# Three attention units of one batch tied behind products of the second expert, in a two-expert kernel

## The chip, the cores and the metric

The kernel runs on one core of one Trainium2 chip. The metric is the time of one execution on the device, in microseconds (us). A core has five engines with a queue each that is worked in order: TensorE (PE in the profile, its weight loads PEld), VectorE (DVE), ScalarE (ACT), GpSimd (POOL) and SyncE (SP), which here issues nearly all DMAs. TensorE's granted clock has two levels, 1.2 and 2.4 GHz; the profile gives it as a share of the higher one.

## What is computed

Attention with a threshold on four batches of 576 tokens, and then two experts, one after the other, on all 2304 tokens:

```python
scores = scale * np.matmul(q, k.transpose(0, 1, 3, 2))        # 4 batches, 8 heads, 576 x 576
thresh = np.max(scores, axis=-1, keepdims=True) - tau
scores = np.where(scores >= thresh, scores, -1000000000.0)
attn = np.exp(scores - max) / (sum + 1e-09)                    # by row
x = np.matmul(attn, v)                                         # 2304 x 512 in all
# first expert, w_in 512 x 2048, w_out 2048 x 512
h = x @ w_in
P = a[0] + a[1] * h + a[2] * h2 + a[3] * h3
Q = 1.0 + np.abs(b[0]) * np.abs(h) + np.abs(b[1]) * h2
x = (P / (Q + 1e-06)) @ w_out
# second expert
h = x @ w_in
g = np.where(h >= 1, h, np.where(h <= -1, 0.0, (h + 1) ** 2 / 4))
out = g @ w_out
```

## The kernel before

Every operand of a product is split into a high and a low half in float16, and a product is made of three: high by high, high by low, low by high.

**The steps.** After the first batch's attention (a form of its own, some 180 us at the start) the experts run as a list of 192 steps. A step is (expert m, batch b, third j of the batch's 576 tokens, chunk i of 256 columns of the 2048): 24 steps are one expert on one batch, and the list alternates, first expert on batch 1, second expert on batch 1, first expert on batch 2, and so on. In this text steps are numbered 0 to 191 and batches 1 to 4 (the code's b is 0 to 3, its m is 0 or 1). So steps 0 to 23 are the first batch's first expert, 24 to 47 its second expert, 48 to 71 the second batch's first expert.

A step has a first product (`first_product`, L889: 24 matmuls of 192 columns into a bank `ph`, of which there are two), elementwise work on its result, and a second product (`second_product`, L905: 24 matmuls into `acc`), which is made LAG = 3 steps later. The elementwise work of the first expert is `rational`: about four ACT operations and five on DVE (L748 to L761; for the first batch one of them goes to ACT, L757, and one to POOL, L758). That of the second expert is `quadratic`: one on ACT (L812), two on DVE (L813, L814). Both end with `split`: a cast on ACT (L210) and a subtraction on POOL (L214).

**Attention of batches 2 to 4.** `attention(b)` is a generator of 17 units: three that prepare (loads, splitting and transposing of q, k and v), then for each of four pairs of heads three units of three rows (`att_rows`), with one more preparation after the second unit of the first two pairs. So a batch has 36 rows of 128 queries. A row goes through all engines in turn: scores on PE (L397 and L398: 4 matmuls, 8 for the last row of a pair) into one PSUM tile `s` of which there is one buffer; scaled and reduced out of it on DVE (L445), bias on ACT (L446), exponential on ACT (L404), threshold on DVE (L405), cast on ACT (L413), low half on POOL (L414, and L416 twice), a transposing DMA on SP (L418: `eT` from `hl`, three buffers each), and the weighted sum on PE (L431: 14 matmuls of 65 columns and less into `pv`). Two rows end in one `normalize` (L466 to L480, with a PE transpose at L471).

**What sets the order.** The code is traced under priorities (`at(t)`: the work of step t), and a list scheduler then fixes each engine's order, priorities and readiness by its own model deciding: work whose operands are ready may be put far ahead of its step where the model sees an engine free. `ATTENTION` (L39) gives for each batch the steps at which the three preparing units begin, at which its rows begin, and at which they end; `spread` puts the units at even distances between. For batch 2 that was 18, 23.65 and 50. A unit traced for step t gets the priority of t - 1.5 (L975 to L977).

**The weights.** The 8 chunks of an expert's weights stay in SBUF (`wc`, 1 MB each, 8 buffers). When the last third of a batch is through with chunk i of one expert, `load_chunk` (L279) loads chunk i of the other one into its place.

## Time and profile before

| | |
|---|---|
| three runs | 1229.77, 1233.0, 1233.4 us (median 1233.0) |
| profiled execution | 1231.83 us, span from first to last instruction 1230.0 us |
| busy share of the span | PE 89%, PEld 80%, DVE 79%, ACT 68%, POOL 45% |
| granted clock, mean | 0.965 |

The rows used are quoted in a section below. They read like this. A row of the windows view gives, for a stretch of the span in us, the busy time of each engine with the number of its instructions, the granted clock and the DMA engines' share. A row of the groups view gives line, engine, operation, tiles written and read, shape, count, then busy us and mean ns, then the engine's idle time just before these instructions and who ended it. A row of the waits view gives who waited for whom, us in total, how many times, and the longest. A row of the timeline gives start, duration, engine, line and operation.

### The profile page before, as it was taken

What the parts mean: (1) busy time and instruction counts of PE and PEld (TensorE: products, weight loads), DVE (VectorE), ACT (ScalarE), POOL (GpSimd) and SP (SyncE); (2) the same over time, 40 slices, a digit from 0 to 9 for tenths busy, and PEclk for the clock granted to TensorE, in tenths of its full rate; (3) what the DMA queues carried; (4) which work ended last, traced back from release to release, by engine and by line L of the source; (5) the groups of instructions that cost most, each with busy time, mean ns of one, the idle gap of its engine ahead of it and who ended that gap; (6) DMA issues with size and microseconds to landing.
All of it is one profiled execution on the core that took longest, in us unless ns stands there. A gap on an engine that the chain in (4) does not pass through costs nothing.

```text
span 1230.0 us, 31762 instructions
## 1 busy us (share of the span) xinstructions
PE 1094.3 (89%) x12636; PEld 989.2 (80%) x12636; DVE 977.6 (79%) x2365; ACT 839.2 (68%) x1532; POOL 553.4 (45%) x698
## 2 busy tenths in 40 slices
PE   2878788588899999998899998988999998999998
PEld 1445555477889988997889898987888998999998
DVE  8887996999997387799995767899987777896432
ACT  2677777798886377788764776888666676775332
POOL 2445455666665166224553564234564652222221
PEclk9889888799999999999999999999999999999999
DMA  7677667644278159734492559333775476007000
GB/s 228 220 224 243 228 243 254 208 116 115 50 191 210 34 117 198 206 101 93 112 277 42 111 93 240 115 78 70 233 177 92 79 193 187 10 2 269 8 14 27
DMA packets 217845, 175.51 MB, mean 143 GB/s; under 512 B 179680, under 2 KB 190944, under 8 KB 209504
## 3 DMA queue, kind: packets, MB, share of 16 engines
q1 hardware_dynamic: 216320, 171.12, 52.5%
q8 instruction: 99, 1.62, 0.5%
q10 hardware_dynamic: 1376, 2.36, 0.5%
q14 instruction: 50, 0.41, 0.1%
HBM read 106.83 MB, written 21.50 MB: 104 GB/s over the span
## 4 chain that ended last, share of the span: by engine, by line
PE 39%; DVE 31%; ACT 10%; DMA 7%; issue 7%; POOL 5%; SPq 1%; ACTq 0%; DVEq 0%; POOLq 0%
PE acc L905 15%; PE ph L889 15%; DMA eT<-hl 3%; DVE e L405 3%; DVE t L755 3%; DVE t L750 2%; DVE sc L445 2%; PE pv L431 2%; DVE t L761 2%; POOL wh L214 2%; PE pv L617 2%; DVE t L760 2%; DVE t L751 2%; DVE t L752 2%; DVE wt L232 1%
## 5 line engine op out<-in xcount | busy, mean ns | idle before, releaser
L905 PE MATMUL acc<-gg,wc 128*128 128x192 f16 x4608 | 426.1, 247 | 12.8 <-POOL gg L214 6.1
L889 PEld LDWEIGHTS <-wc 128*128 128x128 f16 x4608 | 391.2, 99 | 30.0 <-issue 24.3
L905 PEld LDWEIGHTS <-wc 128*128 128x128 f16 x4608 | 385.0, 98 | 13.7 <-issue 12.0
L214 POOL TENSOR_TENSOR gg<-t,gg 128x384 f16<-128x384 f32 x192 | 195.9, 1023 | 382.2 <-ACT gg L210 307.9
L889 PE MATMUL ph<-xT,wc 128*128 128x192 f16 x2304 | 217.8, 252 | 14.4 <-DVE t L752 14.0
L889 PE MATMUL ph<-yT,wc 128*128 128x192 f16 x2304 | 214.4, 247 | 7.1 <-DVE t L814 4.1
L416 POOL TENSOR_TENSOR hl<-e,hl 128x256 f16<-128x256 f32 x216 | 162.5, 772 | 0.0
L210 ACT CAST gg<-t 128x384 f16<-128x384 f32 x192 | 97.1, 508 | 85.2 <-DVE t L814 44.8
L813 DVE SCALAR_TENSOR_TENSOR t<-t,c 128x384 f32<-128x384 f32 x96 | 64.6, 673 | 93.9 <-ACT t L812 92.2
L405 DVE SCALAR_TENSOR_TENSOR e<-sc,nt,e 128x576 f32<-128x576 f32 x108 | 95.1, 881 | 23.3 <-ACT e L404 22.6
L414 POOL TENSOR_TENSOR hl<-e,hl 128x64 f16<-128x64 f32 x108 | 47.4, 439 | 130.3 <-ACT hl L413 121.5
L404 ACT ACTIVATE e<-sc,nt,con 128x576 f32<-128x576 f32 x108 | 93.4, 865 | 4.8 <-POOL hl L416 0.2
L445 DVE TENSOR_SCALAR_CACHE_REDUCE sc<-s 128x576 f32<-128x576 f32 x108 | 80.8, 748 | 16.8 <-PE s L398 16.3
L812 ACT ACTIVATE t<-ph,c 128x384 f32<-128x384 f32 x96 | 64.0, 667 | 41.3 <-PE ph L889 40.9
L413 ACT CAST hl<-e 128x576 f16<-128x576 f32 x108 | 72.1, 668 | 27.4 <-DVE e L405 27.0
L431 PE MATMUL pv<-v,eT 128*128 128x65 f16 (+3 forms) x1680 | 75.1, 194 | 17.4 <-DMA eT<-hl 15.9
L431 PEld LDWEIGHTS <-eT 128*128 128x128 f16 (+1 forms) x1680 | 65.5, 100 | 24.1 <-DMA eT<-hl 18.7
L214 POOL TENSOR_TENSOR wc<-wt,wc 128x256 f16<-128x256 f32 x64 | 54.9, 890 | 61.0 <-ACT wc L210 61.0
L748 ACT ACTIVATE t<-ph,sc 128x384 f32<-128x384 f32 x96 | 55.2, 575 | 38.8 <-PE ph L889 38.2
L753 ACT ACTIVATE t<-t,lc 128x384 f32<-128x384 f32 x96 | 67.7, 708 | 19.6 <-DVE t L750 18.8
L214 POOL TENSOR_TENSOR wh<-wt,wh 128x256 f16<-128x256 f32 x64 | 59.0, 952 | 35.3 <-ACT wh L210 35.2
L750 DVE SCALAR_TENSOR_TENSOR t<-t,qc 128x384 f32<-128x384 f32 x96 | 69.1, 720 | 6.9 <-ACT t L748 6.8
(244 smaller groups left out, 1907.6 us busy)
## 6 DMA issues: line engine op xcount, KB each, us to landing
wc<-scratch SPq DMA_DIRECT2D x56, 1024.0 KB, 6.2
rw<-in_moe_w_in_dram SPq DMA_DIRECT2D x15, 1024.0 KB, 5.6
rw<-in_moe_w_out_dram SPq DMA_DIRECT2D x15, 1024.0 KB, 5.4
scratch<-wc SPq DMA_DIRECT2D x8, 1024.0 KB, 4.5
scratch<-wh SPq DMA_DIRECT2D x16, 512.0 KB, 3.6
rqk<-in_q_dram SPq DMA_DIRECT2D x16, 256.0 KB, 2.9
rqk<-in_k_dram SPq DMA_DIRECT2D x16, 256.0 KB, 3.1
kT<-qkT SPq DMA_DIRECT2D x26, 144.0 KB, 2.6
```

The lines of the kernel that those rows point to most:

```text
L210: A.copy(hi, src)
L214: G.tensor_tensor(lo[:, p], src[:, p], hi[:, p], op=ALU.subtract)
L404: A.activation(e, s, AF.Exp, bias=nb, scale=con[:, 0:1])
L405: V.scalar_tensor_tensor(e, s, th, e, op0=ALU.is_ge, op1=ALU.mult)
L413: A.copy(hi, e)
L416: G.tensor_tensor(lo_w[:, p], e[:, whole][:, p], hi[:, whole][:, p], op=ALU.subtract)
L431: T.matmul(pv[rows, 0:w], eT[:, c, cols], vv[:, h * NT + x if x < NT else H * NT + h, at : at + w], start=(n == 0), stop=(n == len(blocks) ...
L445: V.tensor_scalar(s, banks[:, 0:S], 1.0, -LARGEST, op0=ALU.mult, op1=ALU.max, accum_out=mx)
L750: V.scalar_tensor_tensor(u, u, qc[:, 0:1], u, op0=ALU.add, op1=ALU.mult)
L753: A.activation(r, u, AF.Ln, bias=lc[:, 1:2], scale=lc[:, 0:1])
L889: last = T.matmul(ph[:, f, :], w[:, wx, kt, f * P : (f + 1) * P], rhs, start=(n == 0), stop=(n == 3 * KT - 1))
L905: T.matmul(dst, w[:, wx, f, d * P : (d + 1) * P], gg[:, gx, f, :], start=(i == 0 and f == 0 and n == 0 and d % 2 == 0), stop=(i == NCH - 1 ...
```

## The change

Two things are changed. The table gives batch 2 the steps 18, 24.4 and 49: its three preparing units stay about where they were, its 14 other units begin at step 24.4 in place of 23.65, and end at 49 in place of 50. And each of these 14 units is traced under `tc.issue_after(last)`, where `last` is the last matmul of the first product of the step at which the unit stands. That sets an order and no wait: no matmul of the unit (scores, weighted sums, transposes, sums of a preparation) may stand ahead of that product in PE's queue. Nothing is said of the other engines' instructions, which follow by what they depend on. The arithmetic is the same.

```diff
-ATTENTION = {1: (18, 18 + 32 * 3 / 17, 50), 2: (51, 67, 100), 3: (99, 115, 147)}
+ATTENTION = {1: (18, 24.4, 49), 2: (51, 67, 100), 3: (99, 115, 147)}
+TIED = (1,)
...
                 now[0] = t - 1.5
-                with at(now[0]):
+                with at(now[0]), tc.issue_after(last) if u[1] in TIED and t >= ATTENTION[u[1]][1] else nullcontext():
                     next(atts[u[1]])
```

What it moves shows in the built order. In names, `ph0_0_1_3` is the first product of expert 1, batch 1, third 2, chunk 4 (the code counts from 0), `t0` and `t1` with the same figures its elementwise work, and `s1_0_1_0`, `sc1_0_1_0`, `eT1_0_1_0` belong to batch 2, pair 1, second unit, first row. Lines of the changed kernel are one higher than those of the kernel before.

PE's queue before: the scores of row 1_1_0_0 stand between a second and a first product of the first expert, of step 18.

```order
L397 LDWEIGHTS qkT1_1_3974
L397 MATMUL s1_1_0_0_5039<-qkT1_1_3974 128x512
L398 LDWEIGHTS qkT1_1_3974
L398 MATMUL s1_1_0_0_5039<-kT21_1_3975,qkT1_1_3974 128x512
L397 LDWEIGHTS qkT1_1_3974
L397 MATMUL s1_1_0_0_5039<-qkT1_1_3974 128x64
L398 LDWEIGHTS qkT1_1_3974
L398 MATMUL s1_1_0_0_5039<-kT21_1_3975,qkT1_1_3974 128x64
L905 LDWEIGHTS wc0_6_152
L905 MATMUL acc0_0_1_2941<-gg0_0_1_6_3233,wc0_6_152 128x192
L889 LDWEIGHTS wc0_2_148
L889 MATMUL ph0_0_2_2_3556<-xT0_2_284,wc0_2_148 128x192
```

PE's queue in the changed kernel: the very first scores of batch 2 stand behind the first product of step 24, the second expert's first step.

```order
L890 LDWEIGHTS wc1_0_3774
L890 MATMUL ph1_0_0_0_4145<-yT0_0_2864,wc1_0_3774 128x192
L398 LDWEIGHTS qkT1_0_3668
L398 MATMUL s1_0_0_0_4203<-qkT1_0_3668 128x512
L399 LDWEIGHTS qkT1_0_3668
L399 MATMUL s1_0_0_0_4203<-kT21_0_3669,qkT1_0_3668 128x512
L398 LDWEIGHTS qkT1_0_3668
L398 MATMUL s1_0_0_0_4203<-qkT1_0_3668 128x64
L399 LDWEIGHTS qkT1_0_3668
L399 MATMUL s1_0_0_0_4203<-kT21_0_3669,qkT1_0_3668 128x64
L906 LDWEIGHTS wc0_4_150
L906 MATMUL acc0_0_2_3749<-gg0_0_2_4_3814,wc0_4_150 128x192
```

Counted over the whole order: before, the scores of 14 of the 36 rows, and most of a fifteenth's, stood between steps 7 and 24, 19 rows between 24 and 48, two behind. Now none stands ahead of step 24, 34 stand between 24 and 48, two behind. The weighted sums follow: 17 groups of up to two rows between steps 24 and 48, before 11.

DVE's queue before, in the first expert's steps 9 to 11: three rows' operations (L445, L447, L405) between those of the expert.

```order
L447 TENSOR_SCALAR nt1_0_0_2_4199<-mx1_0_0_2_4198,con1_0_3659 128x1
L405 SCALAR_TENSOR_TENSOR e1_0_0_1_4160<-sc1_0_0_1_4156,nt1_0_0_1_4155,e1_0_0_1_4160 128x576
L755 SCALAR_TENSOR_TENSOR t10_0_1_1_2746<-t10_0_1_1_2746,ka0_1935,t00_0_1_1_2745 128x384
L752 SCALAR_TENSOR_TENSOR t10_0_1_2_2811<-t10_0_1_2_2811,ka0_1935,ph0_0_1_2_2785 128x384
L445 TENSOR_SCALAR sc1_0_1_0_4384,mx1_0_1_0_4382<-s1_0_1_0_4377 128x576
L761 SCALAR_TENSOR_TENSOR t00_0_1_1_2745<-t00_0_1_1_2745,t10_0_1_1_2746 128x384
L750 SCALAR_TENSOR_TENSOR t00_0_1_3_2925<-t00_0_1_3_2925,qc_122 128x384
L751 TENSOR_TENSOR t10_0_1_3_2926<-t10_0_1_3_2926,ph0_0_1_3_2900 128x384
L447 TENSOR_SCALAR nt1_0_1_0_4383<-mx1_0_1_0_4382,con1_0_3659 128x1
L405 SCALAR_TENSOR_TENSOR e1_0_0_2_4204<-sc1_0_0_2_4200,nt1_0_0_2_4199,e1_0_0_2_4204 128x576
```

DVE's queue in the changed kernel, steps 10 to 12: the expert's own operations, and the scale of the third that just ended.

```order
L752 TENSOR_TENSOR t10_0_1_3_2926<-t10_0_1_3_2926,ph0_0_1_3_2900 128x384
L756 SCALAR_TENSOR_TENSOR t10_0_1_2_2811<-t10_0_1_2_2811,ka0_1935,t00_0_1_2_2810 128x384
L753 SCALAR_TENSOR_TENSOR t10_0_1_3_2926<-t10_0_1_3_2926,ka0_1935,ph0_0_1_3_2900 128x384
L762 SCALAR_TENSOR_TENSOR t00_0_1_2_2810<-t00_0_1_2_2810,t10_0_1_2_2811 128x384
L827 TENSOR_REDUCE my0_0_2852<-acc0_0_0_2205 128x1
L191 TENSOR_REDUCE mye0_0_2855<-acc0_0_0_2205 128x1
L751 SCALAR_TENSOR_TENSOR t00_0_1_4_3024<-t00_0_1_4_3024,qc_122 128x384
```

The rows are gone from DVE here, and with them from ACT and POOL. SP's queue in the changed kernel, where the second expert's weights are loaded: the first transposes of batch 2 now stand between these loads.

```order
L280 DMA wc1_2_3939<-scratch1_134 128x4096
L280 DMA wc1_3_4006<-scratch1_134 128x4096
L280 DMA wc1_4_4111<-scratch1_134 128x4096
L419 DMA_TRANSPOSE eT1_0_0_0_4222<-hl1_0_0_0_4217 128x9x128
L280 DMA wc1_5_4201<-scratch1_134 128x4096
L419 DMA_TRANSPOSE eT1_0_0_1_4258<-hl1_0_0_1_4253 128x9x128
L280 DMA wc1_6_4375<-scratch1_134 128x4096
L419 DMA_TRANSPOSE eT1_0_0_2_4302<-hl1_0_0_2_4297 128x9x128
```

Before, the ten rows ahead of the first of these loads had their transposes issued ahead of it too. From step 83 on, PE's order is the same in both kernels.

## Rows read from the trace of the kernel before

**Rows 1.** Windows view: steps 7 to 23, 24 to 37, 38 to 47, 148 to 171.

```profile
core 0: us, PE busy (x) PEld busy (x) DVE busy (x) ACT busy (x) POOL busy (x), PEclk, DMA share, GB/s
263.17:364.57 101.40, 89.20 (x1063) 82.80 (x1063) 100.81 (x253) 89.56 (x175) 67.98 (x79) 0.95 0.45 109
364.57:430.11 65.54, 63.85 (x822) 62.48 (x823) 39.65 (x109) 34.03 (x70) 26.87 (x33) 1.00 0.53 138
430.11:488.97 58.86, 56.56 (x762) 51.55 (x761) 46.35 (x123) 44.81 (x86) 37.42 (x55) 1.00 0.73 155
1035.99:1133.85 97.86, 96.85 (x1169) 96.50 (x1167) 81.84 (x176) 66.44 (x122) 22.75 (x25) 1.00 0.26 90
```

**Rows 2.** First products by source line from 364.57 us on, first and last start.

```profile
L889 PE MATMUL ph<-yT,wc x672: 242/246/257, 364.6 to 638.5; 128*128 128x192 f16 x168
L889 PE MATMUL ph<-xT,wc x576: 243/246/364, 489.0 to 618.8; 128*128 128x192 f16 x192
```

**Rows 3.** Groups of PE, 263.17 to 364.57 us.

```profile
L889 PE MATMUL ph<-xT,wc 128*128 128x192 f16 x408 | 40.8, 262 | 6.4 <-DVE t L752 6.4
```

**Rows 4.** Groups of DVE, 263.17 to 364.57 us.

```profile
L755 DVE SCALAR_TENSOR_TENSOR t<-t,ka,t 128x384 f32<-128x384 f32 x17 | 13.8, 812 | 0.0
L750 DVE SCALAR_TENSOR_TENSOR t<-t,qc 128x384 f32<-128x384 f32 x16 | 13.1, 819 | 0.0
...
L405 DVE SCALAR_TENSOR_TENSOR e<-sc,nt,e 128x576 f32<-128x576 f32 x13 | 11.3, 873 | 0.0
L445 DVE TENSOR_SCALAR_CACHE_REDUCE sc<-s 128x576 f32<-128x576 f32 x14 | 10.4, 743 | 0.0
...
L447 DVE TENSOR_SCALAR nt<-mx,con 128x1 f32<-128x1 f32 x14 | 2.8, 200 | 0.0
```

**Rows 5.** Groups of ACT, and of POOL, 263.17 to 364.57 us.

```profile
L404 ACT ACTIVATE e<-sc,nt,con 128x576 f32<-128x576 f32 x14 | 12.1, 864 | 0.0
...
L413 ACT CAST hl<-e 128x576 f16<-128x576 f32 x13 | 8.7, 671 | 0.7 <-DVE e L405 0.6
...
L446 ACT ACTIVATE nt<-mx,ln_e,con 128x1 f32<-128x1 f32 x14 | 5.4, 386 | 1.2 <-DVE sc L445 1.2
...
L416 POOL TENSOR_TENSOR hl<-e,hl 128x256 f16<-128x256 f32 x26 | 21.6, 849 | 0.0
```

**Rows 6.** Groups of DVE, 1035.99 to 1133.85 us, batch 4 without attention.

```profile
L755 DVE SCALAR_TENSOR_TENSOR t<-t,ka,t 128x384 f32<-128x384 f32 x21 | 13.2, 627 | 5.3 <-ACT t L754 5.3
L750 DVE SCALAR_TENSOR_TENSOR t<-t,qc 128x384 f32<-128x384 f32 x20 | 13.0, 648 | 0.8 <-ACT t L748 0.7
```

**Rows 7.** Groups of DVE, 430.11 to 488.97 us.

```profile
L405 DVE SCALAR_TENSOR_TENSOR e<-sc,nt,e 128x576 f32<-128x576 f32 x15 | 13.9, 926 | 5.5 <-ACT e L404 5.5
L445 DVE TENSOR_SCALAR_CACHE_REDUCE sc<-s 128x576 f32<-128x576 f32 x15 | 11.2, 746 | 1.6 <-PE s L398 1.4
```

**Rows 8.** Timeline from 437.5 us: one row's way from scores to its DMA.

```profile
437.72 0.38 PE L397 MATMUL s<-qkT 128*128 128x512 f16 x1
...
438.18 0.19 PE L398 MATMUL s<-kT,qkT 128*128 128x64 f16 x1
438.21 1.57 PE L905 MATMUL acc<-gg,wc 128*128 128x192 f16 x17
...
440.52 0.60 PE L431 MATMUL pv<-v,eT 128*128 128x65 f16 x14
...
440.96 0.38 PE L397 MATMUL s<-qkT 128*128 128x512 f16 x1
...
446.59 1.30 SPq L418 DMA_TRANSPOSE eT<-hl  x1
```

**Rows 9.** DMA issues, 430.11 to 488.97 us: count, median us to landing.

```profile
eT<-hl SPq DMA_TRANSPOSE x15, 3.4
```

**Rows 10.** DMA issues, 364.57 to 395 us, while weights are loaded.

```profile
eT<-hl SPq DMA_TRANSPOSE x4, 7.2
```

**Rows 11.** Waits of PE, 364.57 to 488.97 us.

```profile
PE pv L431 <- DMA eT<-hl: 1.8, 3, 1.1
```

## The prediction

> **What bounds the kernel now.** I read the page's busy shares first: no engine is full over the span, so the bound changes from stage to stage. Then I cut the span at steps with the windows view and the first products' starts. Step 24 begins at 364.6 us and step 48 at 489.0 us [rows 2]; from 263.17 to 364.57 us stand 408 first-product matmuls, which is 17 steps, 7 to 23 [rows 3]. The same count cuts off steps 38 to 47. The reader is to see two unlike stages there [rows 1]:
>
> Steps 7 to 23 (first expert of batch 1, with some 14 rows of batch 2): DVE is busy 100.81 of 101.40 us. That is the bound. PE is idle for 12.2 us, its clock's mean is 0.95, part of the time at 1.2 GHz, and its first products wait 6.4 us for DVE's L752 [rows 3]. It takes 5.96 us a step.
>
> Steps 24 to 47 (second expert of batch 1, with the other rows): 65.54 + 58.86 = 124.40 us, PE busy 63.85 and 56.56 of these, clock 1.00, DVE only 39.65 and 46.35 [rows 1]. PE is the bound, with 4 us of idle time in all.
>
> For what a step costs with no attention in it, steps 148 to 171 (batch 4) give 97.86 us for 24, that is 4.08 us, PE busy 96.85 [rows 1]. So the change takes work away where DVE is short and PE has room, and puts it where PE is short and DVE has room. The question is what is left over.
>
> **Steps 7 to 23 after the change.** All attention rows leave. From DVE go L405 11.3, L445 10.4, L447 2.8 us [rows 4], and some 6 us in small pieces of `normalize` and of one preparation that the order moves too: about 30 of 100.8 us. L750 and L755 also get shorter: they take 819 and 812 ns here and 648 and 627 ns in batch 4, where POOL is busy for 22.75 of 97.86 us and not 67.98 of 101.40 [rows 1, 4, 6]; half of that difference on 33 instructions is 3 us. DVE keeps about 68 us. From ACT go 12.1 + 8.7 + 5.4 = 26.2 us of 89.56, 63 us stay; POOL loses 21.6 of 67.98 and more [rows 1, 5]. PE's floor is 17 x 4.08 = 69.3 us. So PE becomes the bound, but DVE and ACT stand only 1 to 6 us below it, with the preparation of two pairs and of v among their work, and they hand each step to and fro. I take 73 us. Bounds: 69.3, the floor; and 79.6, 17 steps at the 4.68 us of steps 24 to 37 [rows 1], which do carry rows. Against 101.4 us that is 28 us less (22 to 32).
>
> **Steps 24 to 47 after the change.** By the built order 34 rows' scores stand here and not 19: 15 more. What a row costs here is read from steps 38 to 47, the densest part of this stage: 58.86 - 10 x 3.96 = 19.3 us over bare steps for 15 rows [rows 1, 7], 1.28 us a row, waits and output transposes included (3.96 is 4.08 without the ends of thirds, about 0.9 us each on 8 steps). 15 x 1.28 = 19.2, so 124.4 becomes 143.6 us. The other way round, 24 steps at 5.89 us, the pace of steps 38 to 47 with its 1.5 rows a step, give 141.3. The low bound is the matmuls alone: one row's scores hold PE from 437.72 to 438.21, 0.49 us, one row's weighted sum from 440.52 to 440.96, 0.44 us [rows 8]; 15 x 0.49 + 12 x 0.44 = 12.6 and 137.0 us.
>
> What could make it longer is a row's way through the engines. From its last scores (438.37) to the issue of its transpose (446.59) are 8.2 us, and 3.4 us to the landing [rows 8, 9]: 11.6 us. The new order puts 104 products and two more rows' scores, some 10 us, between the first row's scores and its weighted sum, and for the others mostly 10 to 14 us of work. So the weighted sums will come a little early, as they do now: 1.8 us of waits in three places [rows 11]. PE works in order; behind a waiting weighted sum stand the step's products, behind these ACT's L812 and the rest of the step. For the first rows it is worse: their transposes now stand in SP's queue among the weight loads, and in such a stretch before a transpose took 7.2 us to land and not 3.4 [rows 9, 10]. That is 3.8 us, of which a link or two of the chain shows part: 1.5 us. I take 145 us, that is 20.7 more.
>
> The tie itself is no semaphore, so it adds no wait of its own. The rows' other instructions are moved with them: DVE, ACT and POOL get 15 rows more over these 24 steps, which is the density that steps 38 to 47 already have, with DVE busy 46.35, ACT 44.81 and POOL 37.42 of 58.86 us [rows 1]. That cover is why their cost is nothing here; if it went, the way of a row would lengthen.
>
> **After step 48** two rows' scores are left over in both orders, up to step 83 single rows stand a step earlier or later, and from there the order is the same. I count 0 for it, 3 us either way.
>
> **The sum.** 73 + 145 = 218 against 101.4 + 124.4 = 225.8: 7.8 us less. The profiled execution took 1231.83 us (span 1230.0), so 1224.0; it lies 1.2 us below the median of the runs, 1233.0, against which I give 1225.
>
> **One rule against the trace: the shared port.** L405, with two inputs in SBUF, takes 873 ns in steps 7 to 23 and 926 ns in steps 38 to 47, and L750 takes 819 or 648 ns, as POOL is busy more or less [rows 4, 6, 7]. The Trainium skill (SBUF — State Buffer, Who interferes with whom) says that a DVE instruction with two inputs in SBUF contends with a GpSimd instruction that reads SBUF, and that the later one is blocked. By that rule the contention is not taken away but moved along with the rows; the trace agrees that such instructions stretch. With 0.2 us more on a row's way in each of the 12 links of three rows (below) the sum would be 2.4 us more, 1227; by the rows of steps 38 to 47, which contain the contention already, it is 1225, and I keep that.
>
> **The rivals.**
>
> More gain: both stages come near their bounds, 69.3 + 137.0 = 206.3, or with the pace of steps 38 to 47, 69.3 + 141.3 = 210.6. That is 15 to 19 us less, 1214 to 1218. For it: the earlier half of the stage needs no weights for the next expert, and its PE has little idle time now. Against it: the nearly full ACT, and weighted sums that come early.
>
> No gain: steps 7 to 23 stay near their upper bound of 79.6 us, ACT and DVE handing on too slowly, with 145 us behind: 224.6, 1 us less, 1232. A second way there is the clock: if PE, stopping briefly at many weighted sums, fell to 1.2 GHz now and then, as in steps 7 to 23 with their mean of 0.95, the 145 us would get some 7 us longer, 1232. Steps 38 to 47, with 2.3 us of such stops, show 1.00 throughout [rows 1]. The Trainium skill (TensorE: Matmul & The Clock Gate, A second HAM failure mode: psum-queue depth-cycling) tells of a kernel whose short idle times between groups of matmuls made the clock oscillate; by that rule this rival is what happens, and the trace speaks against it.
>
> Slower: a row's way gets longer. `eT` and `hl` have three buffers each, so about three rows are under way, and 36 rows make some 12 links, each as long as a row's way. Every microsecond more on it costs up to 12 us. The 7.8 us of gain are gone at 0.65 us more a row, and from about 0.95 us the kernel is measurably slower. With 1.3 us more (a third of the 3.8 us that a crowded DMA adds, on every row) it is 1233 - 7.8 + 15.6 = 1241. For it: the DMA engines are busy 0.73 in steps 38 to 47 against 0.53 ahead of them [rows 1]. Against it: most weight loads fall in the stage's first and last quarter, and the way of 11.6 us was measured in a dense part.
>
> That the change doesn't move the rows is excluded by the order.
>
> **Chances.** The forecast, 4 to 13 us less (1220 to 1229): 0.50. More gain (1213 to 1220): 0.17. No gain: 0.13 by the handing on and 0.03 by the clock. Slower: 0.17. A difference under 0.3%, 3.7 us, can hardly be told from none; so faster 0.67, same 0.16, slower 0.17. The range 1213 to 1237 leaves out the worse half of the slower case and the best end.
>
> **What would show it.** Right: step 24 starts near 336 us in place of 364.6; DVE's busy share in steps 7 to 23 falls under 95%, PE's idle time there from 12 us to some 4, its clock to 1.00; steps 24 to 47 take about 145 us, with some 8 to 12 us of waits of L431 for `eT`. The forecast is wrong if steps 7 to 23 stay over 79 us (then ACT or DVE is the bound), if steps 24 to 47 take over 152 us (then the rows' way is longer), or if the clock there is under 0.98.

## The result, and the profile after

| | before | changed |
|---|---|---|
| median of the runs beside each other | 1232.88 us (4 runs, 1229.77 to 1233.4) | 1244.57 us (4 runs, 1242.37 to 1247.12) |
| ratio | | 1.0096, 95% interval 1.007 to 1.0123 |
| span of the profiled execution | 1230.0 us | 1242.0 us |

The change makes the kernel 11.7 us slower, where 7.8 us less were forecast. I cut both profiled executions at the same steps, by the starts of first products. Windows view of the changed kernel: steps 7 to 13, 14 to 19, 20 to 23, then 7 to 23 whole, then 24 to 47.

```profile
core 0: us, PE busy (x) PEld busy (x) DVE busy (x) ACT busy (x) POOL busy (x), PEclk, DMA share, GB/s
265.42:303.07 37.65, 32.96 (x341) 31.12 (x341) 35.52 (x96) 32.86 (x65) 19.16 (x20) 0.91 0.38 110
303.07:328.53 25.46, 24.26 (x291) 23.61 (x289) 23.36 (x43) 19.09 (x39) 13.49 (x13) 1.00 0.01 2
328.53:350.58 22.05, 18.09 (x197) 17.42 (x195) 19.40 (x45) 16.99 (x32) 9.60 (x10) 0.92 0.30 108
265.42:350.58 85.16, 75.31 (x823) 72.15 (x823) 78.28 (x182) 68.94 (x133) 42.25 (x42) 0.94 0.25 77
350.58:501.82 151.24, 136.84 (x1822) 124.33 (x1820) 115.76 (x300) 102.68 (x196) 83.99 (x125) 0.99 0.71 152
```

And the groups view of PE from 265.42 to 350.58 us, which shows that this is 17 steps, as in [rows 3]:

```profile
L890 PE MATMUL ph<-xT,wc 128*128 128x192 f16 x408 | 39.9, 258 | 8.0 <-DVE t L753 7.9
```

Against [rows 1]: steps 7 to 23 fell from 101.40 to 85.16 us, 16.2 less, not 28. Steps 24 to 47 rose from 124.40 to 151.24 us, 26.8 more, not 20.7. What lies behind step 48 takes 740.2 us in place of 741.0. Ahead of step 7 the changed kernel is 2.2 us later; step 0 starts between 181.7 and 185.8 us in profiles of kernels that have the same work ahead of it, so I read nothing from that. -16.2 + 26.8 - 0.8 + 2.2 = 12.0, the difference of the two spans.

In steps 24 to 47 PE is busy 16.4 us more than before (136.84 for 63.85 + 56.56) and idle 10.4 us more (14.40 for 3.99). The waits view of PE for that stretch says at what:

```profile
PE pv L432 <- DMA eT<-hl: 14.2, 12, 3.8
PE xt L472 <- DVE xs L470: 0.2, 1, 0.2
```

Before it was 1.8 us in three places [rows 11]. The chain of work says what that means. Its row of shares by line, for the kernel before, 364.57 to 488.97 us:

```profile
by line: PE ph L889 22.4%; PE acc L905 21.9%; DMA eT<-hl 8.6%; DVE e L405 6.4%; issue 4.5%; PE pv L431 4.5%; DVE t L813 3.7%; DVE sc L445 3.5%; ACT hl L413 2.6%; ACT e L404 2.1%; DVE t L814 1.8%; POOL hl L416 1.7%; DMA rqk<-in_q_dram 1.7%; 
```

The changed kernel, 350.58 to 501.82 us:

```profile
by line: DMA eT<-hl 16.6%; issue 13.9%; POOL hl L417 9.9%; DVE e L406 9.4%; ACT hl L414 4.8%; DVE sc L446 4.2%; DVE t L814 4.1%; POOL gg L215 3.8%; ACT e L405 3.5%; PE ph L890 3.3%; PE acc L906 2.7%; POOL hl L415 2.5%; PE pv L432 2.3%; DVE 
```

This is the plainest view of the change. Before, the two expert products (L889, L905) hold 44% of the chain: PE was the bound. Now they hold 6%, and the chain runs from one row to the next, through L406, L414, L417 and the transpose. The bound has passed from an engine's work to a latency, the time that a row takes on its way.

One row's way shows it. Timeline of the changed kernel, row 1_2_0_1 (scores, its reduction, bias, exponential, threshold, cast, low half, transpose, sum; in between SP's two copies for the preparation of the next pair):

```profile
440.41 0.19 PE L399 MATMUL s<-kT,qkT 128*128 128x64 f16 x1
...
441.95 0.74 DVE L446 TENSOR_SCALAR_CACHE_REDUCE sc<-s 128x576 f32<-128x576 f32 x1
...
442.73 0.39 ACT L447 ACTIVATE nt<-mx,ln_e,con 128x1 f32<-128x1 f32 x1 [0.80 <-DVE sc L446]
...
444.61 0.85 ACT L405 ACTIVATE e<-sc,nt,con 128x576 f32<-128x576 f32 x1
...
446.21 0.81 DVE L406 SCALAR_TENSOR_TENSOR e<-sc,nt,e 128x576 f32<-128x576 f32 x1
...
447.59 0.66 ACT L414 CAST hl<-e 128x576 f16<-128x576 f32 x1
...
448.58 1.82 POOL L417 TENSOR_TENSOR hl<-e,hl 128x256 f16<-128x256 f32 x2
...
451.25 0.49 SPq L373 DMA_DIRECT2D kT<-qkT  x1
...
451.78 0.60 SPq L374 DMA_DIRECT2D kT<-qkT  x1
...
452.54 1.30 SPq L419 DMA_TRANSPOSE eT<-hl  x1
...
455.85 0.61 PE L432 MATMUL pv<-v,eT 128*128 128x65 f16 x14 [1.85 <-DMA eT<-hl]
```

Scores end at 440.60, the transpose is issued at 452.54 and lands after 3.3 us; the sum starts at 455.85, and PE has stood for it for 1.85 us. From scores to landing it is 15.2 us, one of the three longest of the stage, where [rows 8, 9] had 11.6. The low half is ready at 450.40, but SP issues the two copies first, since they are ahead in its queue, and the first of them waits for a transpose of its own. Over the 34 rows whose scores lie in this stage the way from the last scores to the landing is 9.1 to 15.3 us, 12.0 in the median, 12.3 in the mean (worked out row by row from these instructions), and 20 of them take over 11.6. But 11.6 was one row's way. The same working for the 16 rows of the kernel before whose scores lie in steps 38 to 47 gives 10.5 to 16.8 us, 12.1 in the median and 12.6 in the mean: the way of a row is no longer than it was.

What SP's transposes wait for has changed kind. Waits view of SP, the kernel before, 364.57 to 488.97 us:

```profile
SPq L418 <- PE pv L431: 21.9, 4, 12.9
...
SPq L418 <- POOL hl L416: 12.1, 7, 2.3
```

The same of the changed kernel, 350.58 to 501.82 us:

```profile
SPq L419 <- POOL hl L417: 32.8, 21, 3.0
SPq L419 <- ACT hl L414: 22.0, 9, 7.4
SPq L419 <- POOL gg L215: 11.9, 6, 2.6
```

Before, the longest waits of a transpose were for a buffer that a sum had yet to free: rows ran ahead of PE, in steps 24 to 37 above all (three of the four waits, 18.6 us, lie there). In the changed kernel no transpose waits for a sum; they wait for POOL and ACT, and PE waits for them.

### The profile page after: what moved, and what is told of

Same layout as the page of the kernel before. It is cut to its first block, busy times and chain, and to the rows that moved or that the text cites. A ratio compares the mean times of both kernels' runs of the same rounds, so it can differ in the third digit from the quotient of the medians.

```text
span 1242.0 us, 31781 instructions
## 1 busy us (share of the span) xinstructions
PE 1094.3 (88%) x12636; PEld 986.6 (79%) x12636; DVE 989.8 (80%) x2365; ACT 844.9 (68%) x1532; POOL 547.1 (44%) x698
## 4 chain that ended last, share of the span: by engine, by line
PE 39%; DVE 29%; ACT 8%; DMA 8%; issue 7%; POOL 7%; SPq 1%; ACTq 0%; DVEq 0%; POOLq 0%
PE acc L906 15%; PE ph L890 15%; DMA eT<-hl 4%; DVE e L406 3%; PE pv L618 2%; DVE t L756 2%; DVE sc L446 2%; PE pv L432 2%; DVE t L751 2%; DVE t L762 2%; POOL wh L215 2%; POOL hl L417 2%; DVE t L761 2%; DVE t L753 1%; DVE t L752 1%
## 5 line engine op out<-in xcount | busy, mean ns | idle before, releaser
L417 POOL TENSOR_TENSOR hl<-e,hl 128x256 f16<-128x256 f32 x216 | 158.1, 752 | 0.0
L406 DVE SCALAR_TENSOR_TENSOR e<-sc,nt,e 128x576 f32<-128x576 f32 x108 | 99.2, 919 | 31.0 <-ACT e L405 30.1
L415 POOL TENSOR_TENSOR hl<-e,hl 128x64 f16<-128x64 f32 x108 | 43.6, 404 | 136.7 <-ACT hl L414 136.4
L405 ACT ACTIVATE e<-sc,nt,con 128x576 f32<-128x576 f32 x108 | 93.5, 866 | 8.4 <-POOL hl L417 1.8
L414 ACT CAST hl<-e 128x576 f16<-128x576 f32 x108 | 72.2, 668 | 31.2 <-DVE e L406 28.6
L756 DVE SCALAR_TENSOR_TENSOR t<-t,ka,t 128x384 f32<-128x384 f32 x96 | 70.1, 731 | 10.1 <-ACT t L755 9.7
L751 DVE SCALAR_TENSOR_TENSOR t<-t,qc 128x384 f32<-128x384 f32 x96 | 70.4, 734 | 8.2 <-ACT t L749 6.8
```

The source lines that it names most:

```text
L405: A.activation(e, s, AF.Exp, bias=nb, scale=con[:, 0:1])
L406: V.scalar_tensor_tensor(e, s, th, e, op0=ALU.is_ge, op1=ALU.mult)
L414: A.copy(hi, e)
L417: G.tensor_tensor(lo_w[:, p], e[:, whole][:, p], hi[:, whole][:, p], op=ALU.subtract)
L751: V.scalar_tensor_tensor(u, u, qc[:, 0:1], u, op0=ALU.add, op1=ALU.mult)
L756: V.scalar_tensor_tensor(s, s, ka[:, 0:1], r, op0=ALU.add, op1=ALU.mult)
```

## The experiments

Each was compared with the kernel before on the same chip, run again beside it (median 1232.9 us beside the changed kernel, 1234.0 to 1234.8 beside the others; each ratio is to its own). The table gives medians and ratios, and from the profiled execution of each the time at which step 7 starts and how long the three stretches behind take (differences of first products' starts; the last one ends with the span). These stretches are of one execution, which in four rows lies far from the median of its kernel: 7.9 us below it for the kernel before with free sums, 4.6 below for no loads, 8.8 above for four eT with later sums, 4.1 above for preparation tied with batch 3 later.

| kernel | us | ratio, 95% | step 7 at | 7-23 | 24-47 | from 48 |
|---|---|---|---|---|---|---|
| before | 1232.9 | | 263.2 | 101.4 | 124.4 | 741.0 |
| changed | 1244.6 | 1.0096 (1.007-1.0123) | 265.4 | 85.2 | 151.2 | 740.2 |
| tie alone | 1239.7 | 1.0027 (1.0-1.0054) | 262.7 | 85.6 | 147.2 | 739.7 |
| table alone | 1234.3 | 0.9979 (0.995-1.0008) | 264.9 | 100.6 | 129.4 | 737.5 |
| DVE in place of POOL | 1247.4 | 1.0083 (1.0047-1.0118) | 263.3 | 81.7 | 156.4 | 745.4 |
| free sums | 1224.7 | 0.9914 (0.9885-0.9943) | 266.7 | 85.5 | 138.4 | 732.1 |
| before, free sums | 1228.7 | 0.9949 (0.9915-0.9982) | 264.1 | 97.5 | 124.3 | 732.8 |
| sums three rows later | 1247.9 | 1.0126 (1.0077-1.0175) | 265.9 | 85.0 | 150.1 | 742.0 |
| four eT, sums later | 1237.5 | 1.0025 (0.999-1.006) | 266.4 | 91.5 | 148.0 | 738.4 |
| no loads | 1243.4 | 1.0049 (1.0018-1.008) | 264.4 | 83.6 | 148.3 | 740.7 |
| preparation tied | 1235.0 | 1.0007 (0.9988-1.0027) | 260.8 | 83.1 | 148.4 | 740.7 |
| preparation tied, free sums | 1223.8 | 0.9917 (0.9896-0.9938) | 262.2 | 82.7 | 142.8 | 732.2 |
| preparation tied, four eT | 1236.6 | 1.0014 (0.9996-1.0032) | 257.9 | 89.9 | 151.3 | 736.7 |
| tied from step 18 | 1246.8 | 1.0107 (1.0068-1.0145) | 281.4 | 80.2 | 147.8 | 735.2 |
| the same, preparation tied | 1251.2 | 1.014 (1.0123-1.0156) | 254.8 | 104.4 | 156.6 | 732.7 |
| changed, batch 3 later | 1255.2 | 1.0173 (1.0139-1.0207) | 266.5 | 85.1 | 153.2 | 747.5 |
| preparation tied, batch 3 later | 1249.7 | 1.013 (1.009-1.017) | 262.7 | 82.9 | 151.0 | 755.4 |
| before, batch 3 later | 1233.3 | 0.9994 (0.9974-1.0013) | 263.8 | 101.7 | 124.4 | 742.5 |

**The two halves of the change.** My theory after the result was that PE stands at sums which the tie places too near behind their scores; the rival, that the new table or the order behind it does it.

```diff
-ATTENTION = {1: (18, 24.4, 49), ...
+ATTENTION = {1: (18, 18 + 32 * 3 / 17, 50), ...     # tie alone
```

> The tie on batch 2's units, with the old table (18, 23.65, 50). If the tie is what moves the rows, PE's order is nearly that of the changed kernel (no row ahead of step 24, 33 rows in steps 24 to 47) and the time is too: 1241 to 1248 us, steps 7 to 23 about 85 us, steps 24 to 47 about 150 us. Rival: the later end of the table (50 for 49) spreads the rows enough to save the waits for transposes, steps 24 to 47 take under 146 us and the time is 1238 us or less.

```diff
-TIED = (1,)
+TIED = ()                                           # table alone
```

> The new table (18, 24.4, 49) with no tie. In the built order the rows stand where they stood before (15 of 36 ahead of step 24), so by the theory that the tie is the change the time is that of the kernel before, 1229 to 1236 us, with steps 7 to 23 at about 101 us and DVE busy over 98% of them. Rival: the earlier end of the rows (49) brings a part of the loss by itself, over 1238 us.

The tie does it: with it alone steps 7 to 23 take 85.6 us as in the changed kernel, steps 24 to 47 147.2, and the sums wait 12.4 us. The table alone leaves the rows where they were, steps 7 to 23 at 100.6 us and the kernel's time unchanged; its steps 24 to 47 are 5.0 us longer than before, but there PE is idle for 4.2 us as before and busy 4.8 us more, at a granted clock of 0.97 for 1.00. The tie alone costs only 0.3% and not 1%, a little less than I expected: 4 us in steps 24 to 47, and 3 us ahead of step 7 in the profiles, which is the scatter of that stretch.

**What the waits cost.** In both kernels the sums of batch 2 read a constant tile, so that no sum waits for a transpose.

```diff
-weighted(pvs[t][:, ab], slice(0, P), eT, slice(0, P), vv, h + ab, ab)
+weighted(pvs[t][:, ab], slice(0, P), ones if b == 1 else eT, slice(0, P), vv, h + ab, ab)
...
```

> The changed kernel, but batch 2's weighted sums read a constant tile in place of the transposed row, so that they wait for no transpose; everything else of a row, its transposes included, is still made (left out: the weights of batch 2's sums). Theory A: the 14.2 us that PE waits at weighted sums in steps 24 to 47 are what this stage lost, and these steps fall from 151.2 to 134 to 139 us and the time to 1228 to 1233 us. Theory B: the row's other work (DVE, ACT, POOL) holds the experts' products up as well, and as one wait goes another comes: steps 24 to 47 stay over 144 us.

> The kernel before with batch 2's weighted sums reading a constant tile of ones (left out: the weights in these sums), as in the earlier run with the changed kernel (1224.7 us). In both the rows of batch 3 stand in the same order up to step 83, so the difference is the move of batch 2's rows without any wait for transposes. Theory A (free sums also bring the other order of batch 3, worth 8 to 10 us, and the move itself is worth nothing): steps 48 to 83 take 180 to 184 us and not 189, steps 7 to 47 stay at 222 to 226 us, the kernel 1222 to 1228 us. Theory B (free sums matter only where the rows are tied): 1230 to 1234 us, and the move without waits is then worth 6 to 9 us.

Windows of the changed kernel with free sums, steps 7 to 23 and 24 to 47:

```profile
core 0: us, PE busy (x) PEld busy (x) DVE busy (x) ACT busy (x) POOL busy (x), PEclk, DMA share, GB/s
266.67:352.14 85.47, 75.26 (x823) 72.17 (x823) 78.75 (x182) 68.93 (x133) 42.04 (x42) 0.94 0.25 78
352.14:490.59 138.45, 135.49 (x1883) 125.98 (x1881) 113.03 (x310) 103.34 (x200) 86.10 (x125) 1.00 0.72 160
```

The same two of the kernel before with free sums:

```profile
core 0: us, PE busy (x) PEld busy (x) DVE busy (x) ACT busy (x) POOL busy (x), PEclk, DMA share, GB/s
264.14:361.62 97.48, 86.22 (x1022) 81.20 (x1022) 95.38 (x237) 84.06 (x164) 60.70 (x71) 0.95 0.40 102
361.62:485.96 124.34, 122.48 (x1623) 115.39 (x1623) 94.07 (x245) 86.00 (x167) 67.24 (x100) 1.00 0.63 150
```

Without the waits steps 24 to 47 take 138.45 us and not 151.24, PE idle for 3.0 us. So the waits, and what they set back, are worth 12.8 us of that stage: 11.4 of idle time, and 1.4 of PE's busy time, with a clock of 1.00 for 0.99. And the chain is PE's again (shares by line from 352.14 to 490.59 us; L893 and L909 are the two products here):

```profile
by line: PE ph L893 24.0%; PE acc L909 23.8%; PE pv L435 7.6%; issue 4.7%; PE s L401 4.6%; PE s L402 4.3%; DMA qkT<-qk 4.3%; DVE e L409 3.5%; POOL hl L420 2.2%; DVE sc L449 2.1%; ACT hl L417 1.8%; DMA rqk<-in_k_dram 1.6%; DVE t L817 1.5%; D
```

The second pair of windows tells more. Between these two kernels, which have batch 3 in the same order up to step 83, the rows' move takes 12.0 us out of steps 7 to 23 and puts 14.1 us into 24 to 47. So in these two profiles the move is worth nothing even with no wait at all, 2 us too much. The medians (1224.7 and 1228.7 us) put the tied one 4 us ahead, but the intervals of the two ratios overlap, and the profile of the second is of one of its two fastest executions: that the move without waits is worth some us is neither shown nor excluded. 1228.7 lies between what theories A and B gave; the stages lie just outside A's ranges (221.8 us for steps 7 to 47; 185.1 from step 48 to the start of step 83). Of the 20 us by which free sums beat the changed kernel, 8 lie behind step 48 (732 for 740 us). The kernel before has 733 for 741 there with free sums, in that one execution; for its median, 5 us better than without them, that isn't shown.

**Can the waits be taken away in earnest?** First without more space: sums traced three rows later.

```diff
+            if len(late) == 3:
+                late.pop(0)()
...
+            row = partial(att_sum, b, pr, t, ab, eT, vv, h, pvs)
+            if b == 1:
+                late.append(row)
+            else:
+                row()
```

> The changed kernel, but a row's weighted sum of batch 2 is traced only ahead of the scores of the third row behind it (the last three at the batch's end). The three buffers stay, so each row can start its transpose just after the sum three rows earlier. By the built order the PE work between a row's scores and its sum rises little: median 12.2 us in place of 11.4, 17 rows in place of 22 below the 11.6 us of a row's way. Theory (PE stands in order at sums that come too early): waits of sums for the transposes fall from 14.2 us to 6 to 11, steps 24 to 47 take 144 to 149 us and not 151.2, the kernel 1236 to 1243 us. Rival (more rows make everything slower, by DMA and DVE contention, wherever the sums stand): the waits may move but steps 24 to 47 stay at 150 to 153 us, the kernel at 1243 to 1247.

The theory's waits are missed, 13.1 us, and the times are the rival's: 150.1 us for the stage, and 1247.9 us, just over its range. The work between scores and sums had grown by under 1 us, too little to count, and 1 us was about what the waits fell. Then with a fourth buffer of `eT` and sums four rows later, so that 15.5 us of PE work lie between:

```diff
-N_TEMP, N_POLY, N_WT, N_WH, N_GG, N_ROW, N_SC = 5, 3, 3, 2, 4, 3, 2
+N_TEMP, N_POLY, N_WT, N_WH, N_GG, N_ROW, N_SC = 5, 3, 3, 1, 4, 3, 2
...
-eT = ap.tile([P, C, P], F16, name="eT" + name, tag="eT", bufs=N_ROW)
+eT = ap.tile([P, C, P], F16, name="eT" + name, tag="eT", bufs=N_ROW + 1)
...
```

> The changed kernel with four buffers of eT and the weighted sums of batch 2 traced four rows behind their scores; the space comes from one buffer less of the tile on which the experts' weights are prepared (wh, 1 in place of 2), which belongs to the steps up to 20 and may cost there. By the built order the PE work between a row's scores and its sum is 15.5 us in the median (11.4 in the changed kernel), and 3 rows stay below 11.6 us. Theory (early sums and too few buffers): waits of sums for transposes under 5 us in steps 24 to 47, which take 138 to 143 us; without what the lost weight buffer costs ahead of step 24 the kernel takes 1226 to 1234 us. Rival (contention): steps 24 to 47 over 147 us although hardly a sum waits.

Waits view of its PE, steps 24 to 47:

```profile
PE s L398 <- DVE sc L448: 8.4, 8, 1.8
PE pv L432 <- DMA eT<-hl: 1.3, 1, 1.3
```

Sums hardly wait, and the stage still takes 148.0 us: now the scores wait 8.4 us for DVE's reduction to free the one buffer `s`. My theory was right on the waits and wrong on what they are worth here: behind the link that is taken away stands the next one of the same row. The stage's time is the one that I gave under the rival, contention; whether DVE's reductions come late because so many rows stand there is not shown. This execution is the slowest of ten, so the waits are to be read from it rather than the time.

**Are the weight loads to blame?** The eight loads of the second expert's weights ahead of batch 1 are left out.

```diff
-            chunks[1 - m, i] = load_chunk(1 - m, i)
+            chunks[1 - m, i] = load_chunk(1 - m, i) if n else chunks[m, i]
```

> The changed kernel without the eight loads of the second expert's weights ahead of its first batch (left out: these weights; the second expert works on batch 1 with the first one's). It tells whether the transposes that stand among 1 MB loads are what makes the sums wait. Theory A (loads and transposes share the DMA engines): transposes of steps 24 to 35 land in the 3.3 us of the later ones and not in up to 8 us, the sums' waits there fall from 7.3 us to under 4, steps 24 to 35 take 64 to 68 us and not 72.1, steps 36 to 47 stay near 79. Theory B (the sums stand too near behind their scores, whatever the DMA does): waits there stay at 6 us or more and the steps at 70 to 73 us. By A the kernel takes 1235 to 1240 us, by B 1242 to 1247.

DMA issues of steps 24 to 35, the changed kernel (count, median us to landing):

```profile
eT<-hl SPq DMA_TRANSPOSE x15, 3.9
```

Without the loads:

```profile
eT<-hl SPq DMA_TRANSPOSE x15, 3.3
```

The landings shorten as theory A has them, from 3.9 us in the median to 3.3 and from at most 8.0 to 5.1, but the waits there only from 7.3 to 5.8 us and the steps from 72.2 to 70.2, and the kernel stays at 1243.4 us. That is theory B, its waits a little under the 6 us, with a share of some 2 us for the loads.

**Why steps 7 to 23 fell so little.** The first suspect was POOL's own product of batch 1 (L759), which I had not counted.

```diff
-        g = rational(ph, i, consts, name, b == 0) if m == 0 else quadratic(ph, i, consts, name)
+        g = rational(ph, i, consts, name, False) if m == 0 else quadratic(ph, i, consts, name)
```

> The changed kernel, but batch 1's first expert makes the one product that it has on POOL (after an ACT operation) on DVE, in one operation, as the other batches do. In the changed kernel steps 7 to 23 take 85.2 us where I forecast 73, with DVE busy 78.3 us. Theory A: POOL's product, at 1.2 us each, stretches DVE's operations with two inputs in SBUF (874, 783 and 748 ns against 627, 555 and 648 ns in batch 4) and lengthens each step's chain; without it these fall under 680 ns, and steps 7 to 23 to 80 us or less. Theory B: what is slow are the tail of the weights' staging, the preparations and the ends of thirds; DVE only gets 17 times 0.6 us more, and these steps take 85 us or more. Steps 24 to 47 stay at 151 us under both.

Groups of DVE in steps 7 to 23 of the changed kernel:

```profile
L756 DVE SCALAR_TENSOR_TENSOR t<-t,ka,t 128x384 f32<-128x384 f32 x18 | 15.6, 874 | 0.9 <-ACT t L755 0.5
L762 DVE SCALAR_TENSOR_TENSOR t<-t,t 128x384 f32<-128x384 f32 x19 | 14.9, 783 | 2.6 <-POOL t L759 2.6
L751 DVE SCALAR_TENSOR_TENSOR t<-t,qc 128x384 f32<-128x384 f32 x17 | 12.7, 748 | 1.2 <-ACT t L749 1.1
L753 DVE SCALAR_TENSOR_TENSOR t<-t,ka,ph 128x384 f32<-128x384 f32 x17 | 10.3, 606 | 0.1
L752 DVE TENSOR_TENSOR t<-t,ph 128x384 f32<-128x384 f32 x18 | 9.8, 542 | 0.0
```

The group of POOL's product in the same stretch:

```profile
L759 POOL TENSOR_TENSOR t<-t 128x384 f32<-128x384 f32 x18 | 21.7, 1205 | 23.9 <-ACT t L758 22.5 <-PE acc L906 1.0
```

Groups of DVE with that product on DVE (L761):

```profile
L761 DVE SCALAR_TENSOR_TENSOR t<-t,qc 128x384 f32<-128x384 f32 x18 | 12.6, 698 | 0.0
L756 DVE SCALAR_TENSOR_TENSOR t<-t,ka,t 128x384 f32<-128x384 f32 x18 | 12.3, 681 | 2.2 <-ACT t L755 2.2
L751 DVE SCALAR_TENSOR_TENSOR t<-t,qc 128x384 f32<-128x384 f32 x17 | 11.3, 662 | 0.0
L753 DVE SCALAR_TENSOR_TENSOR t<-t,ka,ph 128x384 f32<-128x384 f32 x17 | 10.3, 604 | 0.1
L762 DVE SCALAR_TENSOR_TENSOR t<-t,t 128x384 f32<-128x384 f32 x18 | 10.1, 563 | 0.0
L752 DVE TENSOR_TENSOR t<-t,ph 128x384 f32<-128x384 f32 x17 | 9.2, 542 | 0.0
```

With the rows gone L756 did not get shorter, as I had it, but longer (874 ns, before 812 [rows 4]), and L751 fell from 819 to 748 ns only: POOL's product stretches them. Without it L756 falls from 874 to 681 ns, L762 from 783 to 563, L751 from 748 to 662. The Trainium skill (SBUF — State Buffer, Who interferes with whom) says that DVE instructions with two inputs in SBUF contend with GpSimd instructions that read it; the trace agrees, with 13 to 39% on such an instruction here. L752 and L753, which read one input from PSUM (`ph`), take 542 and 606 ns with the product beside them and 542 and 604 without it. But the product itself costs DVE 12.6 us, so DVE's busy time in the stage does not fall (79.24 us for 78.28); it stands idle less, and the stage gains 3.5. That is 81.7 us, between what the two theories gave and nearer to A's. The kernel is none the faster, since steps 24 to 47 take 156.4 us there, which neither theory had: the waits are as before (14.5 us), but PE is busy 141.60 us for 136.84, at a clock of 0.96 for 0.99.

The second suspect was the preparation of batch 2, which stays in steps 5 to 9. Here it is tied as well, and moves to steps 19 to 23.

```diff
-                with at(now[0]), tc.issue_after(last) if u[1] in TIED and t >= ATTENTION[u[1]][1] else nullcontext():
+                with at(now[0]), tc.issue_after(last) if u[1] in TIED and t >= ATTENTION[u[1]][0] else nullcontext():
```

> The changed kernel with the three preparing units of batch 2 tied too, so that they stand behind steps 19, 21 and 23 and not 5, 7 and 9. Theory (steps 7 to 13 are long because DVE, 35.5 of 37.65 us busy, does some 7 us of preparation there): steps 7 to 13 take 30 to 33 us; steps 14 to 23, 47.5 us in the changed kernel, get 2 to 7 us of it back; the kernel 1240 to 1245 us. Rival (handing each step to and fro between ACT, DVE and POOL, or the weights, sets the pace there, not the sum of DVE's work): steps 7 to 13 stay at 36 us or more and the later steps still lengthen, the kernel over 1246 us.

Windows of steps 7 to 13, 14 to 19, 20 to 23:

```profile
core 0: us, PE busy (x) PEld busy (x) DVE busy (x) ACT busy (x) POOL busy (x), PEclk, DMA share, GB/s
260.84:293.86 33.02, 28.82 (x339) 27.85 (x339) 30.50 (x49) 26.74 (x50) 19.68 (x18) 1.00 0.04 17
293.86:318.80 24.94, 24.94 (x305) 24.92 (x303) 20.40 (x44) 20.73 (x39) 12.69 (x12) 1.00 0.01 2
318.80:343.96 25.16, 17.41 (x204) 16.85 (x203) 25.16 (x80) 20.84 (x41) 9.97 (x12) 0.98 0.78 244
```

As expected: steps 7 to 13 take 33.0 us and not 37.7; 3.1 of the 4.6 us come back in steps 20 to 23, where DVE is now busy for all of 25.16 us. The clock changes too: in steps 7 to 13 it is 1.00 for 0.91, and PE's busy time falls by 4.1 us, DVE's by 5.0; how much of the 4.6 us is due to each, this run doesn't tell apart. Steps 14 to 19 have PE busy in every microsecond, 4.16 a step: there the floor is reached. The kernel comes to 1235.0 us, the same as before, and better than expected: another 4.6 us lie ahead of step 7, 2.1 of them ahead of step 0, and 2.8 in steps 24 to 47, where the sums wait 9.1 us.

With this and free sums together the question was whether the gains add.

> The preparing units tied, and batch 2's weighted sums reading a constant tile of ones in place of the transposed weights, so that they wait for no transpose (left out: the weights in batch 2's sums). It bounds what the move of the rows can bring. Theory (the two losses are separate): the kernel takes some 9 us less than with free sums alone (1224.7), 1214 to 1219 us, with steps 7 to 23 at 82 to 85 us and 24 to 47 at 135 to 139 us. Rival (the preparing units pay only through the sums' waits, which are gone here): 1222 to 1227 us. Either way the two stages together stay at 217 us or more, where the forecast wanted 218 with the waits in it.

They don't: 1223.8 us, the rival's number, 83 + 143 us in the two stages. And this with four buffers of `eT`, the nearest thing to it that computes all:

> The two edits together that each took something back: the preparing units tied (1235.0 us alone), and four buffers of eT with sums four rows behind their scores (1237.5 us alone, paid with one buffer wh less). Theory (behind the waits for the transposes stands the next link of a row's way, the one buffer s and the two of sc and e): sums wait under 3 us in steps 24 to 47, but scores wait 4 to 9 us for DVE's L448; that stage takes 144 to 149 us, the kernel 1228 to 1236 us. Rival (the transposes alone were the matter): the stage takes 137 to 143 us, the kernel 1220 to 1228 us.

1236.6 us, as before within 0.3%. The sums' waits are 4.3 us, the scores' 3.0, and a new one, of a transpose on PE for DVE's L481, is 4.7: once more the next link. The stage, at 151.3 us, is over what either theory gave.

**Fewer rows in the second stage.** Tied from step 18, some 30 rows lie in steps 24 to 47; the second kernel ties the preparing units too.

```diff
-ATTENTION = {1: (18, 24.4, 49), ...
+ATTENTION = {1: (12, 18, 49), ...
```

> The changed kernel with batch 2's rows tied from step 18 and not from step 24 on (table 12, 18, 49): 6 rows stand behind steps 18 to 23, where the changed kernel runs at PE's pace, and some 30 between 24 and 48. The PE work between scores and sums does not change (median 11.0 us). Theory (each tied row waits some 0.4 us at its sum, and each costs 1.28 us of its own in the second stage): steps 24 to 47 take 144 to 148 us, steps 7 to 23 rise from 85 to 88 to 93 us, since their DVE is full again; the kernel 1240 to 1246 us. Rival (the second stage is only too dense, at 34 rows in 24 steps, and is relieved by more than its share): steps 24 to 47 take under 142 us, steps 7 to 23 no more than 88, the kernel under 1236 us.

> Batch 2 tied from step 18 on (table 12, 18, 49), now with the preparing units tied too, from step 12: without that the preparing units stood at steps 0 to 3, the first batch's attention and steps 0 to 6 took some 16 us more, and the gain of the middle was lost. Theory: that loss goes (steps 0 to 6 at 79 us and not 88.7, start of step 0 near 183 us and not 192.7), steps 7 to 23 take 82 to 88 us with the preparing units back in them, steps 24 to 47 stay at 146 to 149 us; the kernel 1230 to 1237 us, about as before. Rival (with fewer rows the second stage comes loose): steps 24 to 47 under 142 us, the kernel under 1228 us.

Steps 24 to 47 are hardly shorter, 147.8 us, as the theory had it, though steps 7 to 23 take no more than 80.2 us with six rows in them, where it had 88 to 93; the preparing units, now in steps 0 to 3 and the attention ahead, cost 16 us before step 7 against the changed kernel, and the time, 1246.8 us, is just over the range given. With these units tied, steps 14 to 23 take 76.7 us in place of 47.5, and the kernel 1251.2. My expectation for that kernel failed: DVE is busy 75.02 of these 76.71 us, 14.2 of them with work on the second expert's weights (L231 to L233), which in the changed kernel and in the two kernels with one of these edits ends ahead of step 7. The rest of the 29 us I did not follow.

**The order of batch 3.** From step 48 to the start of step 83 it took 181 to 183 us in three kernels where the list scheduler had put batch 3's rows later (free sums, tied from step 18, table alone), and 189 and 191 us in the kernel before and the changed one. The expectations call this stretch steps 48 to 83. Here the table puts these rows later.

```diff
-2: (51, 67, 100)
+2: (54, 68, 100)      # changed kernel, with and without the preparation tied; the kernel before: (53, 67, 100)
```

> The changed kernel with batch 3's units begun three steps later and its rows one (table 54, 68, 100), which puts batch 3's rows about where the kernels with the shorter steps 48 to 83 have them (59, 61, 63, 65, 67, 68, 69, 72, .. in place of 58, 60, 60, 62, 63, 64, ..); batch 2's order is the same. Theory A (that order costs 8 to 10 us): steps 48 to 83 take 180 to 185 us and not 191.3, the kernel 1234 to 1238 us, the rest unchanged with its 14 us of waits in steps 24 to 47. Theory B (those steps are longer because of what the late rows of batch 2 leave behind): they stay at 188 us or more, the kernel 1241 to 1246.

> The same table for batch 3 (54, 68, 100) with batch 2's preparing units tied too, which alone gave 1235.0 us with the old order of batch 3 (steps 48 to 83: 190.6 us). Theory A: 180 to 185 us there, the kernel 1225 to 1229 us, faster than the kernel before. Theory B: 188 us or more, the kernel 1233 to 1237.

> The kernel before, untied, with batch 3's units begun two steps later (table 53, 67, 100): its rows of batch 3 stand behind steps 60, 61, 63, 65, 66, 67, 68, 72, 73, .. and not 57, 59, 60, 61, 62, 63, ... Theory A: steps 48 to 83 fall from 189.1 to 180 to 185 us, the kernel to 1225 to 1230 us, all without the change. Theory B: they stay at 187 us or more, the kernel at 1231 to 1236.

Theory A falls. In the kernel before the stretch takes 185.3 us, at the edge of A's range: steps 48 to 71 get 7.4 us shorter (124.6 for 132.0), but the steps behind give it back, and the whole is the same, as B has it. In the two others the stretch stays at 190 us, as B has it, but the whole is longer than either theory gave: all that lies behind step 48 takes 7 and 15 us more. Why, and what free sums win behind step 48, is then not explained by batch 3's order alone, and stays open.

No version that computes everything is shown to beat the kernel before: the best, the table alone, is 0.2% faster, with an interval that takes in none.

## Why the prediction was wrong

**What bounds the kernel**: right. Steps 7 to 23 were DVE's and 24 to 47 PE's, and the rows went from the one to the other as the order said.

**Steps 7 to 23, 73 us**: wrong by 12 us. The step that failed is that DVE keeps 68 us; it keeps 78.28. Seven of the ten are the expert's own five operations: 59.1 us before, 56 expected, 63.3 measured, for 89 instructions and not 85; the four more are some 3 us of it, and the operations themselves got no shorter, 0.71 us each for 0.70. I took batch 4's durations as where they would go, but batch 4 has no product on POOL; with that product on DVE the five take 53.2 us for 87. The other three of the ten I did not follow. And I took 17 steps as alike. They are three stretches: steps 14 to 19 do run near the floor (25.46 us, where six steps at 4.08 are 24.5), in steps 7 to 13 DVE is busy 35.52 of 37.65 us, the preparation among it, and in steps 20 to 23 PE waits 4.0 of 22.05 us for DVE's L753. PE's idle time, forecast at some 4 us, was 9.85, and its clock, forecast at 1.00, was 0.94; it came to 0.91 and 0.92 in the two outer stretches, part of the time at 1.2 GHz, and to 1.00 between. The clock alone is not what held the stage: with the preparation tied, at 1.00, 1.00 and 0.98, PE is busy 4.1 us less, and the stage is only 2.0 us shorter. Of the upper bound, 79.6 us, I had said that the forecast is wrong beyond it; so it is, and by DVE.

**Steps 24 to 47, 145 us**: 151.24, just inside the 152 that I gave as the limit. The matmuls were sized right: 13.0 us more PE time for 15 rows with free sums (135.49 for 122.48), 0.87 a row, against 0.84 from [rows 8]. The term that failed is the wait: 8 to 12 us, of which 1.5 over the pace of steps 38 to 47. I read 1.28 us a row there as if it held the waits of the new order too. It held 1.8 us of waits for 15 rows, 0.12 a row: two more, of 1.5 and 1.7 us, at sums of rows whose scores stand in those steps, fall behind step 48, where I did not look, and no sum of the rows of steps 24 to 37, which ran ahead of PE, waited at all. In the new order the wait for transposes is 14.2 us for 34 rows, 0.42 a row, and 12.8 us of the stage go with it.

**After step 48, 0**: right in the sum, 740.2 for 741.0, but with some luck: steps 48 to 71 take 3.9 us more (135.9 for 132.0), and those behind 4.7 less.

**The rivals.** "Slower: a row's way gets longer" comes near the time, with 1241 us against a measured 1244.6, and had 17%; but that is in part luck. Sums do wait for a row's way, as it says, and yet the way did not get longer (12.3 us in the mean of 34 rows, 12.6 before in 16 rows, one of which waits 3.3 us for a buffer); 11.6 was one row's way, 0.7 us under the new mean and 1.0 under the old. And the three buffers were not the link: no transpose waits for a sum to free one, and a fourth, with later sums, moved the waits on to the scores. What sets the pace is where the sum stands on PE, 11.4 us of work behind the scores in the median (the built order's instructions by their durations in the trace), against a way of 12.0. I had both numbers ("the others mostly 10 to 14 us of work", "11.6 us") and called it a little early. On a queue worked in order, what a row lacks is PE's idle time: twelve waits in 34 rows. The new order is not much worse by the row than the dense part of the old one: those 16 rows, with 12.2 us of PE's work behind their scores in the median (from the trace; 11.7 so counted in the changed kernel), wait 5.0 us at their sums, 0.31 a row for 0.42. It is worse because 34 rows stand so, where before the others ran ahead. The clock rival came in small: PE's clock in this stage fell to 1.2 GHz once, from 494.74 to 498.16 us, in the longest of the twelve stops, which ends at 495.46. The mean is 0.99 and the price within the 1.4 us of busy time named above; with POOL's product on DVE the mean is 0.96 and PE is busy 4.8 us longer. The oscillation of which the Trainium skill tells (TensorE: Matmul & The Clock Gate, A second HAM failure mode: psum-queue depth-cycling) is not what this trace shows: one fall, in a stop of 3.8 us, and none in the eleven shorter ones.

**The shared port.** I weighed it as a cost that moves with the rows. In steps 7 to 23 it did not leave with them: the expert's operations with both inputs in SBUF stayed as long beside POOL's own product as they had been beside the rows and that product.

**The chances.** 67% for faster rested on a gain of 28 us against a loss of 20.7, and both came from rows of other stretches. With the bounds that I had myself, 79.6 and 152, the sum was 232, 6 us slower; that end was as well founded as the middle.

## What to carry to other kernels

Work that ran ahead of the full engine cost it only its own instructions here; tied to its place, each piece also cost what its way lacked. Before tying, set the engine's work between issue and use against the whole way, measured on many rows and not on one, and ask for a margin and not for equality. When a wait is taken away, look at the next link of the same piece before counting the gain: here removing the wait for the transpose uncovered the one bank of scores. And a stage that loses a load falls only where that load was the bound; cut it into its parts before giving it another stretch's pace.

## What the runs showed of the hardware

A DVE instruction with two inputs in SBUF, 128 x 384 in float32, took 563 to 681 ns without POOL's product in the stage and 748 to 874 ns with it; with one of the inputs in PSUM it took 542 to 606 ns in both. In steps 24 to 35 a transposing DMA landed after 3.2 us at the least, 3.9 in the median and 8.0 at the most among loads of 1 MB, and after 3.2, 3.3 and 5.1 us with these loads left out. TensorE kept 2.4 GHz through eleven stops of up to 2.6 us in steps 24 to 47 of the changed kernel and fell to 1.2 GHz for 3.4 us in the twelfth, of 3.8 us; in steps 20 to 23, where it is busy 18.09 of 22.05 us, with stops of 1.8 and 2.1 us, it fell as well, and the mean came to 0.92.
